# A fused attention and gated convolution kernel: q and k of group 5 loaded ahead of w_out, groups 3 to 5 run through the prologue, pair loop begun at group 6

## The chip, the cores and the metric

The kernel runs on one core of one Trainium2 chip. The metric is the device time of one execution in microseconds (us), where less is better. A run that lies more than 1.5% above the fastest of the same kernel is called slow here, and the other runs fast. Where the text says "span", it is the length of the profiled execution, about 1.8 us shorter than its device time (222.6 us for 224.45 in the profiled run of the kernel before).

## The reference, cut to what matters

```python
batch, n_heads, seq, head_dim = 8, 12, 448, 64         # d_model = 768
scores = q @ k.T / 8                                    # per batch and head, causal mask
attn   = softmax(scores) @ v                            # (8, 12, 448, 64)
x      = attn with heads joined                         # (8, 448, 768)
gate   = sigmoid(causal_depthwise_conv(x, conv_w))      # 5 taps
out    = (gate * (x @ w_val)) @ w_out                   # (8, 448, 768), float32
```

## The kernel before

The work is cut into 24 groups of four heads; three groups make one batch. For each group the kernel computes scores and exps in two stages, multiplies by v ("attention"), normalises, and runs the convolution that gives the gate. For each batch and each third of the columns there is a "value product" (`val`: x times w_val, times the gate), and for each pair of batches 14 "output tiles" (`project`: times w_out). Value products and output tiles have no fixed place: they fill the gaps in which TensorE would wait for ScalarE's exps. `plan` and `vals_in` say how many go into which gap. Names that end in `_ps` are the banks that TensorE writes its results to: `sc_ps` for scores and convolutions, `av_ps` and `den_ps` for attention and its denominators, `z_ps` and `den_ps` for products and output tiles.

Loads of q, k, w_val and w_out are issued by GpSimd, which also masks the exps with selects and casts v. Its timeline shows them in the order of the program, so a load behind a select waits for that select's exps: in the kernel before, a select starts at 38.63 us after 3.17 us of waiting for exps, and q of group 6, which the program has behind it, is issued at 43.35 us.

```python
    def next_outs(count, banks, tiles=1):     # output tiles; tiles=4 cuts each of the six matmuls into four narrow ones
        ...
    def first_half(n):
        if n < N:
            exps(n, 0)                        # scores on TensorE, exps on ScalarE, two selects on GpSimd
            transposes(n + 1)                 # q, k of the next group, on VectorE
            cast_v(n)                         # on GpSimd
            load_v(n + 3)
            for m in {4: (6, 7), 5: (8,), 6: (9,), 7: (10, 11)}.get(n, (n + 4,)):
                load_qk(m)                    # issued by GpSimd
    ...
    exps(2, 1, 2)
    load_qk(4)
    for c in range(NE):
        load_wo(c)                            # the six pieces of w_out
    load_qk(5)
    cast_v(1, nc.vector)
    load_v(4)
    values(1)                                 # attention and normalisation
    cast_v(2, nc.vector)
    load_v(5)
    conv((0, 1), sc_banks)
    values(2)
    transposes(3)
    next_val((z_ps, den_ps))
    exps(3, 0)
    next_val((z_ps, den_ps))
    conv((2,), [av_ps])
    exps(3, 1)
    ...
    plan = {2: (2, 0, 1, 0, 1), 3: (2, 0, 0, 0, 0), 4: (0, 1, 2, 1, 2), 5: (2, 0, 0, 0, 0)}
    vals_in = {2: (), 3: (2, 4), 4: (0,), 5: (2, 4)}
    for p in range(2, N // 2 + 1):            # one pair of groups per turn
        n = 2 * p
        ...
        first_half(n)
        gap(0, (den_ps, z_ps))
        second_half(n)
        values(n - 1)
        gap(1, (z_ps,), 4)                    # output tiles in gaps 1 and 3 are cut in four
        if p == 2:
            swap_wv()                         # an exchange of rows of w_val inside SBUF, four DMAs
        first_half(n + 1)
        gap(2, (den_ps, z_ps))
        second_half(n + 1)
        if n < N:
            values(n)
        gap(3, (z_ps,), 4)
        conv((n - 2, n - 1) if p > 2 else (n - 1,), sc_banks)
        gap(4, (den_ps, z_ps, av_ps[0]))
```

The softmax here doesn't subtract the row's maximum and nothing guards it: scores larger than these inputs give would overflow.

## Time and profile before

The time was 225.32 us, the median of three runs (224.0 to 225.81). The points below are the starts of a group's scores on TensorE and the end of the span, from the trace.

| point | us | stretch | us |
|---|---|---|---|
| scores of group 3 | 31.6 | start to group 3 | 31.6 |
| scores of group 6 | 52.3 | group 3 to 6 | 20.7 |
| scores of group 12 | 97.0 | group 6 to 12 | 44.7 |
| end of the span | 222.6 | group 12 to the end | 125.6 |

TensorE is busy 94% of the span, so the time is moved only by what makes TensorE stand, by its clock, or by more work. The list of TensorE's waits of this kernel gives, for each kind, the total in us, how many there were, and the longest. Two lines of it matter later.

```profile
PE sc_ps L181 <- ACT pt L190: 1.6, 5, 0.6
...
PE sc_ps L241 <- issue: 0.5, 1, 0.5
```

The first says that all waits of scores for ScalarE's exps together cost 1.6 us: the gaps are well filled. The second is one wait inside a convolution for which the profile names no other engine and no transfer ("issue").

### The profile page before, as it was taken

The numbers are of one execution on the slowest core, as the hardware profiler recorded it, in microseconds if no ns is written. First come the engines' busy times: TensorE is split into PE (matmuls) and PEld (weight loads), VectorE is DVE, ScalarE is ACT, GpSimd is POOL, SyncE is SP. The second block draws the span as 40 slices with busy tenths as digits, with TensorE's granted clock in tenths as the row PEclk, the third lists the DMA queues.
The fourth block names the chain that finished last, engine by engine and source line by source line (L and its number), as shares of the span: only waits on it lengthen the run. The fifth ranks groups of instructions, "written<-read, shape, count | busy, mean of one in ns | idle before, by whom it ended". The sixth has DMA issues, their size and how long they took to land.

```text
span 222.6 us, 8748 instructions
## 1 busy us (share of the span) xinstructions
PE 208.4 (94%) x3821; PEld 114.1 (51%) x3822; DVE 139.4 (63%) x251; ACT 139.7 (63%) x178; POOL 111.4 (50%) x192
## 2 busy tenths in 40 slices
PE   7997889987999999999999999999999999989992
PEld 3344434544455545545655655555555556546551
DVE  6747686558878754978828828749568476260400
ACT  2496316877666868667677777777677776406041
POOL 7299953893884736817717636557255155000000
PEclk9999699999999999999999999999999999999999
DMA  5999999899999885984885977758934210302333
GB/s 92 176 196 223 220 215 203 169 171 268 223 271 203 172 180 209 239 157 90 161 235 109 229 212 134 154 192 165 193 141 135 88 59 3 144 0 89 128 137 149
DMA packets 57696, 36.37 MB, mean 163 GB/s; under 512 B 46133, under 2 KB 54069, under 8 KB 57658
## 3 DMA queue, kind: packets, MB, share of 16 engines
q1 hardware_dynamic: 48922, 22.44, 37.6%
q0 software_dynamic: 8736, 13.37, 34.6%
q8 instruction: 30, 0.49, 0.9%
q14 instruction: 8, 0.07, 0.1%
HBM read 37.76 MB, written 11.01 MB: 219 GB/s over the span
## 4 chain that ended last, share of the span: by engine, by line
PE 77%; ACT 8%; DVE 7%; DMA 3%; issue 2%; POOL 1%; DVEq 0%; ACTq 0%; POOLq 0%
PE den_ps L263 12%; PE z_ps L263 11%; PE sc_ps L181 11%; PE z_ps L285 11%; ACT pt L190 7%; PE sc_ps L241 7%; PE den_ps L285 6%; PE av_ps L215 5%; PE den_ps L215 4%; PE av_ps L285 3%; PE z_ps L134 3%; DMA kb<-in_k_dram 3%; PE sc_ps L285 2%; DVE x L228 2%; DVE dt L222 1%
## 5 line engine op out<-in xcount | busy, mean ns | idle before, releaser
L190 ACT ACTIVATE pt<-sc_ps 128x1024 bf16<-128x1024 f32 x96 | 92.9, 1022 | 34.1 <-PE sc_ps L181 32.6
L194 POOL TENSOR_SCALAR_AFFINE_SELECT pt<-pt 128x512 bf16<-128x512 bf16 x24 | 16.0, 668 | 66.5 <-ACT pt L190 66.5
L285 PEld LDWEIGHTS <-gv 128*32 128x32 bf16 (+1 forms) x624 | 31.6, 97 | 22.3 <-issue 4.6
L263 PEld LDWEIGHTS <-wv 128*128 128x128 bf16 x288 | 26.4, 98 | 26.0 <-issue 3.2
L181 PE MATMUL sc_ps<-qt,kt 32*128 32x64 bf16 (+3 forms) x768 | 35.0, 277 | 2.1 <-ACT pt L190 1.6
L285 PE MATMUL z_ps<-wo,gv 128*32 128x384 bf16 (+1 forms) x462 | 33.2, 326 | 0.8 <-DVE gv L266 0.8
L200 POOL TENSOR_SCALAR_AFFINE_SELECT pt<-pt 128x512 bf16<-128x512 bf16 x48 | 30.2, 660 | 7.0 <-ACT pt L190 7.0
L181 PEld LDWEIGHTS <-kt 32*128 32x128 bf16 x768 | 18.4, 93 | 27.4 <-issue 17.2
L263 PE MATMUL z_ps<-x,wv 128*128 128x448 bf16 x138 | 30.2, 353 | 0.7 <-DVE x L228 0.7
L263 PE MATMUL den_ps<-x,wv 128*128 128x448 bf16 x138 | 30.3, 354 | 0.2
L266 DVE SCALAR_TENSOR_TENSOR gv<-gate,den_ps 128x448 bf16<-128x448 f32 x23 | 14.1, 612 | 24.6 <-PE den_ps L263 24.6
L228 DVE TENSOR_TENSOR x<-av_ps,rb 128x448 bf16<-128x448 f32 x48 | 27.7, 619 | 2.6
L248 ACT ACTIVATE gate<-sc_ps 128x896 f32<-128x896 f32 x23 | 19.9, 915 | 14.9 <-PE sc_ps L241 14.9
L222 DVE STREAM_TRANSPOSE dt<-den_ps 128x448 f32<-128x448 f32 x24 | 15.5, 644 | 18.4 <-PE den_ps L215 18.4
L215 PE MATMUL av_ps<-pt,vb 128*32 128x448 bf16 (+3 forms) x768 | 25.3, 274 | 0.7 <-DVE vb L86 0.7
L165 DVE STREAM_TRANSPOSE qt<-qb 128x448 uint32<-128x448 uint32 x24 | 22.8, 950 | 4.7 <-DMA qb<-in_q_dram 4.5
L290 ACT ACTIVATE ob<-z_ps 128x384 f32<-128x384 f32 x29 | 14.3, 493 | 15.8 <-PE z_ps L285 15.8
L165 DVE STREAM_TRANSPOSE kt<-kb 128x448 uint32<-128x448 uint32 x24 | 22.3, 930 | 1.8 <-DMA kb<-in_k_dram 1.8
L86 POOL CAST vb<-vf 128x1024 bf16<-128x1024 f32 x21 | 21.8, 1036 | 0.0
L215 PEld LDWEIGHTS <-vb 128*32 128x32 bf16 x768 | 16.3, 98 | 6.4 <-DVE vb L86 0.9
L241 PE MATMUL sc_ps<-x,cwd 32*32 32x448 bf16 x920 | 17.7, 369 | 1.8 <-DVE x L228 0.9
L266 DVE SCALAR_TENSOR_TENSOR gv<-gate,z_ps 128x448 bf16<-128x448 f32 x23 | 14.1, 614 | 7.9 <-PE z_ps L263 7.9
(46 smaller groups left out, 174.9 us busy)
## 6 DMA issues: line engine op xcount, KB each, us to landing
out_dram<-ob SPq DMA_DIRECT2D x27, 384.0 KB, 4.1
vf<-in_v_dram SPq DMA_DIRECT2D x72, 128.0 KB, 5.6
qb<-in_q_dram POOLq DMA_DIRECT2D x24, 224.0 KB, 4.8
kb<-in_k_dram POOLq DMA_DIRECT2D x24, 224.0 KB, 6.0
vf<-in_v_dram SPq DMA_DIRECT2D x24, 64.0 KB, 5.3
wv<-in_moe_w_val_dram POOLq DMA_DIRECT2D x12, 96.0 KB, 6.0
wo<-in_moe_w_out_dram POOLq DMA_DIRECT2D x6, 192.0 KB, 8.8
wv<-wv SPq DMA_DIRECT2D x4, 96.0 KB, 7.6
```

The lines of the kernel that those rows point to most:

```text
L86: engine.tensor_copy(out=t, in_=vfs.pop(n))
L165: nc.vector.transpose(out=t.bitcast(U32).rearrange("p (b s) -> p s b", s=T), in_=qks.pop((name, n)).rearrange("p s d -> p (s d)").bitcast( ...
L181: nc.tensor.matmul(out=sc_ps[h // 2][:, h % 2, c0:c0 + nq], lhsT=kt[r, e, k0:k0 + 128], rhs=qt[r, e, q0:S], start=e == 0, stop=e == 1, ski ...
L190: nc.scalar.activation(out=pt[:, 2 * hp:2 * hp + 2, 512 * stage:512 * (stage + 1)], in_=sc_ps[hp], func=AF.Exp, scale=D ** -0.5)
L200: nc.gpsimd.affine_select(out=pt[:, :, c:c + 128], in_=pt[:, :, c:c + 128], compare_op=ALU.is_ge, fill=0.0, base=0, pattern=[[0, G], [1, 1 ...
L215: nc.tensor.matmul(out=o, lhsT=w, rhs=pt[:, h, col:col + nq], start=i == 0, stop=i == 3, skip_group_check=True, tile_position=(0, 32 * i_out))
L228: nc.vector.tensor_tensor(out=x[:, dh, 4:S + 4], in0=av_ps[dh][:, 0:S], in1=r, op=ALU.mult)
L241: nc.tensor.matmul(out=banks[u][i // 2][32 * j:32 * (j + 1), 0:S], lhsT=cwd[r, 2 * version(n) + dh, t], rhs=xs[n % 8][r, dh, t:t + S], sta ...
L248: nc.scalar.activation(out=gates[n], in_=sc_ps[u][:, :, 0:S], func=AF.Tanh, scale=0.5)
L263: nc.tensor.matmul(out=o[e][:, 0:S], lhsT=wv_sb[version(NG * b + cg)][:, ce, f:f + 128], rhs=xs[(NG * b + cg) % 8][:, ce, 4:S + 4], start= ...
L266: nc.vector.scalar_tensor_tensor(out=gv[g][:, e, S * (b % 2):S * (b % 2 + 1)], in0=gates[NG * b + g][:, e], scalar=1.0, in1=o[e][:, 0:S], ...
L285: nc.tensor.matmul(out=o[w * j:w * (j + 1), 0:384], lhsT=gvs[p][g][:, dh, 128 * m + w * j:128 * m + w * (j + 1)], rhs=wo_sb[c][:, f], star ...
```

## The change

Its intent, as the code shows it: let q and k of group 5 arrive before w_out, run groups 3 to 5 straight through to their attention in the prologue, and let the regular loop begin at group 6. It also moves two v casts to other places and computes the last two of the six contraction steps of the first value product late.

```diff
-            for m in {4: (6, 7), 5: (8,), 6: (9,), 7: (10, 11)}.get(n, (n + 4,)):
+            for m in {6: (8, 9), 7: (10,), 8: (11, 12)}.get(n, (n + 4,)):
 ...
     load_v(3)
+    cast_v(1, nc.vector)
     exps(1, 1, 2)
     keep_clock(3)
+    exps(2, 0, 2)
     load_wvs(4)
-    load_qk(3)
-    exps(2, 0, 2)
     values(0)
     exps(2, 1, 2)
+    cast_v(2, nc.scalar)
+    load_qk(3)
     load_qk(4)
+    values(1)
+    conv((0, 1), sc_banks)
+    values(2)
+    transposes(3, v_f[1])
+    ...
+    next_val((z_ps, den_ps), 2)
+    conv((2,), [av_ps])
+    exps(3, 0)
+    transposes(4)
+    cast_v(3)
+    load_v(6)
+    load_qk(5)
+    next_val((z_ps, den_ps))
+    exps(3, 1)
     for c in range(NE):
         load_wo(c)
-    load_qk(5)
 ... (the old order of groups 1 to 3 removed)
     next_val((z_ps, den_ps))
+    exps(4, 0)
+    ...
+    values(3)
+    transposes(5)
+    exps(4, 1)
+    next_outs(1, (z_ps,))
+    exps(5, 0)
+    ...
+    load_qk(7)
+    values(4)
+    next_outs(1, (z_ps,), 4)
+    exps(5, 1)
+    transposes(6)
+    next_outs(2, (z_ps, den_ps))
+    values(5)
+    conv((3, 4), sc_banks)
+    swap_wv()
+    next_outs(1, (z_ps,))

-    plan = {2: (2, 0, 1, 0, 1), 3: (2, 0, 0, 0, 0), 4: (0, 1, 2, 1, 2), 5: (2, 0, 0, 0, 0)}
-    vals_in = {2: (), 3: (2, 4), 4: (0,), 5: (2, 4)}
-    for p in range(2, N // 2 + 1):
+    plan = {3: (0, 1, 0, 1, 2), 4: (1, 2, 0, 1, 1), 5: (0, 1, 0, 0, 0)}
+    vals_in = {3: (0, 2, 4), 4: (), 5: (0, 2)}
+    for p in range(3, N // 2 + 1):
```

## The prediction

> **What bounds the kernel now.** I read the page's head first: busy shares, then the forty slices of 5.6 us.
>
> ```profile
> PE 208.4 (94%) x3821; PEld 114.1 (51%) x3822; DVE 139.4 (63%) x251; ACT 139.7 (63%) x178; POOL 111.4 (50%) x192
> ...
> PE   7997889987999999999999999999999999989992
> ...
> PEclk9999699999999999999999999999999999999999
> DMA  5999999899999885984885977758934210302333
> ```
>
> TensorE is the bound at 94%. What it lacks lies in the first eleven slices and in the tail. Its clock fell once, in the fifth slice, and the DMA engines are full for the first 60 us. Next the order of instructions of both kernels: the first 17 us match on TensorE, and from the scores of group 12 (97.0 us of the span now) both have the same order to the end, with 8 value products and 14 output tiles done by then. So the remaining 125.5 us are the same work, and the change can only move the moment at which group 12 begins.
>
> Then the timeline of TensorE from 17 to 55 us, where the idle time before a piece is in brackets.
>
> ```profile
> 21.21 1.06 PE L215 MATMUL av_ps<-pt,vb 128*32 128x448 bf16 x32 [0.71 <-DVE vb L86]
> ...
> 23.45 2.59 PE L241 MATMUL sc_ps<-x,cwd 32*32 32x448 bf16 x79 [0.89 <-DVE x L228]
> ...
> 31.62 0.63 PE L181 MATMUL sc_ps<-qt,kt 32*128 32x448 bf16 x16
> ...
> 39.42 1.17 PE L285 MATMUL den_ps<-wo,gv 128*128 128x384 bf16 x6 [0.18 <-DVE gv L266]
> ...
> 51.21 1.14 PE L285 MATMUL den_ps<-wo,gv 128*128 128x384 bf16 x6 [1.20 <-DVE dt L222]
> 52.28 0.64 PE L181 MATMUL sc_ps<-qt,kt 32*128 32x448 bf16 x16
> ```
>
> The gaps that the change aims at: 0.71 us for the cast of v, 0.89 us for x of group 1, and 1.20 us at 51.2, whose releaser stood behind the k transpose of group 6. The lines at 31.62 (group 3 starts), 39.42 (first output tile) and 52.28 (group 6 starts) are my reference points. The windows of 3.4 us around the clock's fall:
>
> ```profile
> 20.40:23.80 3.40, 1.80 (x49) 0.87 (x42) 3.23 (x7) 0.56 (x1) 3.40 (x7) 1.00 1.19 230
> 23.80:27.20 3.40, 3.25 (x103) 1.77 (x98) 1.33 (x3) 1.10 (x2) 3.40 (x7) 0.50 1.19 214
> ```
>
> After a window with TensorE 53% busy (1.80 of 3.40) comes one at clock 0.50, and then 1.00 again: 1.7 us of work lost. Last, the DMA issues. These two are the sixth w_out piece (issued 30.57) and k of group 5 (issued 33.65), from narrow windows:
>
> ```profile
> wo<-in_moe_w_out_dram POOLq DMA_DIRECT2D x1, 192.0 KB, 9.7
> ```
> ```profile
> kb<-in_k_dram POOLq DMA_DIRECT2D x1, 224.0 KB, 9.1
> ```
>
> So w_out is complete at 30.57 + 9.7 = 40.3 us, just when the first output tile, at 39.42, comes to its sixth matmul. w_out is not early in the old kernel; it is just in time. k of group 5 stands behind it and lands at 33.65 + 9.1 = 42.8; its transpose holds TensorE for 0.30 us at 43.8. That is what the reordering of the loads can win directly.
>
> [...] the DMA share is 1.16 to 1.22 in every 5 us stretch from 20 to 40. [...]
>
> **The change, part by part.**
>
> *Early waits.* The second v cast moves ahead of the first normalisation on VectorE (its data are there: 0.9 MB had moved on the v queue by 15 us) and the third goes to ScalarE, where a 128x1024 pass takes 1.02 us and which is free after 20.9. That removes the 0.71 us wait and brings x of group 1 forward by about 0.6. x of group 2 then comes near 27.7 instead of 29.9, and computing the last two of six contraction steps late hides what remains. But group 3 cannot start before its k is here. On GpSimd, q and k of group 3 now stand behind two more selects (0.63 + 0.41 and 1.2 us) and a later w_val: sel(2) from 20.1, four w_val issues of 0.55 to 23.3, sel(2) to 24.5, then q at 24.5, k at 25.05. k needs at least 4.0 us (what k of group 0 took on empty queues), more likely 5, plus 0.95 for its transpose: group 3 starts at 30.2 to 31.3, I take 30.9 against 31.62. The convolution of group 2 (1.1 us) is done before it instead of after. Gain here: 0.7 + 1.1 = 1.8 us.
>
> *q, k ahead of w_out.* This is the step that decides. GpSimd is in order. Group 3's scores at 30.9, exps on ScalarE done at 30.9 + 2.7 = 33.6, two selects to 34.65, cast (1.04) to 35.65, and only then q and k of group 5 (now 32.3 and 33.65). Second scores at 30.9 + 0.6 + 2.4 (a value product is 1.24 + 1.14) = 33.9, exps to 36.6, selects to 37.9, then six w_out issues of 0.54: 37.9 to 41.2, against 27.1 to 31.1 now. Meanwhile the software queue has nothing between k of group 4 (about 32) and 37. k of group 5, issued at 36.2 with 4.3 to 5.8 us to land (its range on lightly loaded queues in this trace), is here near 41; w_out follows at the pace of now, where k of group 4 landed at 26.57 + 6.6 = 33.2 and w_out was complete 7.1 us later. So w_out is complete near 48.1, between 46 and 50.
>
> TensorE reaches the first output tile after scores, value product, scores, value product, scores (30.9 to 37.5), attention of group 3 (1.5, with a short wait for its selects) and the second scores of group 4, held by the exps to 40.2. It stands from 40.2 to about 48.3, less the matmuls whose weights have come: 7 us idle. The clock goes to half, and comes back one busy window later: 1.5 us more.
>
> *From the first output tile to group 6.* Scores 0.6, attention 1.42, output 1.03, scores 0.6, two outputs 2.1, attention 1.42 after 0.8 of waiting for the denominator bank (its copy stands behind two exps on ScalarE), convolution 1.24, output 1.03: 10.2 us. Group 6 starts at 48.3 + 10.2 + 1.5 = 60.0, against 52.28. By then one attention (1.42) and one output tile (1.03) more are done, 2.5 us.
>
> *Group 6 to group 12.* Now 44.8 us with about 1.4 us of short waits. Afterwards 2.5 us less work, but the places between two users of the score banks are filled less: scores of group 9 follow each other with nothing between (two exps of 1.02 less 0.3: 1.7 us), the convolution of groups 8 and 9 is followed at once by scores (two gates, 1.73 us), and four further places have one output tile of 1.03 where 1.7 to 2 are to be covered (0.6 to 0.9 each, 3 in all). That is 6.4 us of waits for 1.4. So 44.8 - 2.5 + 5 = 47.3, and group 12 starts at 107.3 instead of 97.0.
>
> Sum by terms: early gain -1.8, stall +7 (arrival at the tile is already 0.8 later because 2 us of work and some waits now stand before it), clock +1.5, thinner filling +5, removal of the old waits between 42 and 52 (0.3 + 0.6 + 1.2) -2.1: +9.6 us by terms, +10.3 by the walk. Every wait in it is taken at its full length, and hand walks add up waits that in fact overlap (a later TensorE finds ScalarE done), so I take three quarters: +7.5, that is 232.8 us.
>
> **The rivals.**
>
> *The early gain stands and w_out is in time.* Speaking for it: somebody placed the output tiles and chose the new plan with care, and the loads of v for groups 4 and 5 are held back on purpose by a dependence on the q transpose of group 3, which frees DMA time. Against it: all issues on GpSimd stand behind selects that wait for exps of group 3. Even with every step at its shortest (k landing in 4.0 us, w_out at 1 us a piece) w_out is complete at 45.3 and the tile is reached at 39.1. If I am wrong nonetheless, 1.8 + 2.1 us are won: 221 to 222 us.
>
> *The stall comes but is given back.* TensorE stands, the DMA queues run ahead, later waits go. Against: from 97 us on TensorE is at 20.00 of 20.00 in four stretches of 20 us, so there is no slack to give back; only the 1.4 us between groups 6 and 12 could be. Time about 227 to 229.
>
> *ScalarE becomes the bound between groups 6 and 12*, because scores, gates and output copies meet with no other TensorE work between. It is 63% busy; it holds TensorE only at the six places counted. With the full sum: 235.
>
> **Range and chances.** The shortest variant of each step gives a stall of 5 us and half of the thinner filling: +2 to +4, 228. The longest gives w_out at 50 and two cold windows: +13, 238. Range 226.5 to 238. The threshold for slower is 229.8. I give slower 0.73, same 0.17, faster 0.10; the last two are for the case that my order of GpSimd's work or the pace of its queue is wrong, and for the care that the author evidently took.
>
> **What would show it.** The chain of waits should hold a DMA of w_out at 40 to 48 us; the timeline of TensorE a wait of several us inside the first output tile's six matmuls, with a clock of 0.5 after it; w_out's first issue at 37 to 38.5; group 6's scores starting near 58 to 60 and group 12's at 102 to 107; waits of about 1.5 us on exps and gates at group 9's second and group 12's first scores; from group 12 to the end 125.5 us as before. It would be wrong if w_out is complete by 42, or if group 12 starts before 98.

## The result, and the profile after

The changed kernel took 247.85 us (median of four runs, 244.75 to 250.73) against 224.84 us (224.0 to 225.81) of the kernel before: a ratio of 1.093, with a 95% interval of 1.0814 to 1.1046. It is slower, by about 21 to 23 us. A ratio is the mean time of one kernel's fast runs over that of the other's fast runs in the same rounds, so it is not quite the ratio of the medians quoted beside it. The first profile of the changed kernel fell on a slow run, so I ran the same kernel again (run `after_again`, 246.38 us, ratio 1.0924), and all lines of the changed kernel below are from that profile of a fast run.

The head of the page of the changed kernel:

```profile
PE 216.0 (88%) x3893; PEld 116.1 (47%) x3894; DVE 138.9 (57%) x251; ACT 141.8 (58%) x180; POOL 111.0 (45%) x192
...
PE   7896986388996977995999988999999999998993
...
PEclk9999999759997999999799999999999999999998
DMA  5999998967559539979179398487792430111324
```

TensorE has 72 more matmuls than before (3893 for 3821) and 72 more weight loads, and is busy 88% instead of 94%. A slice is now 6.1 us. The row PE shows a 3 in the eighth slice (43 to 49 us), and PEclk a 7, 5 there and after it, and further 7s in the 13th and the 20th slice. DMA is nearly full through the eighth slice and then falls to 3 and 1 in places.

GpSimd's timeline of the changed kernel (start, length, and in brackets the idle time before with what ended it):

```profile
34.78 0.63 POOL L197 TENSOR_SCALAR_AFFINE_SELECT pt<-pt 128x512 bf16<-128x512 bf16 x1 [7.01 <-ACT pt L193]
...
37.26 0.54 POOL L67 DMA_DIRECT2D kb<-in_k_dram  x1
...
38.97 3.20 POOL L105 DMA_DIRECT2D wo<-in_moe_w_out_dram  x6
```

GpSimd stood idle for 7 us, waiting for the exps of group 3, and the loads behind that select waited with it. The six w_out issues begin at 38.97 us; before, the first five began at 27.09. TensorE's timeline of the changed kernel has the price:

```profile
31.95 0.63 PE L184 MATMUL sc_ps<-qt,kt 32*128 32x448 bf16 x16 [0.74 <-DVE kt L168]
...
44.78 0.32 PE L290 MATMUL z_ps<-wo,gv 128*128 128x384 bf16 x1 [3.57 <-DMA wo<-in_moe_w_out_dram]
...
49.88 0.48 PE L290 MATMUL z_ps<-wo,gv 128*128 128x384 bf16 x1 [0.70 <-DMA wo<-in_moe_w_out_dram]
...
63.26 0.37 PE L184 MATMUL sc_ps<-qt,kt 32*128 32x448 bf16 x2
...
115.25 0.37 PE L184 MATMUL sc_ps<-qt,kt 32*128 32x448 bf16 x2 [1.01 <-ACT gate L251]
```

In the kernel before, group 12 started so:

```profile
97.01 0.64 PE L181 MATMUL sc_ps<-qt,kt 32*128 32x448 bf16 x16
```

These lines answer the reference points of the prediction. Group 3 starts at 31.95 us (31.62 before). TensorE reaches the first output tile at 41.2 (44.78 less the 3.57 of waiting), and its sixth matmul begins only at 49.88. Group 6 starts at 63.26 (52.28 before), group 12 at 115.25 (97.01 before). About a microsecond of such a difference can be chance: the idle matmuls ahead of group 1's scores, where all programs of this document are still equal, continue at 10.88 us in the profile of the kernel before, at 11.96 in this one, and between 10.8 and 12.3 in all 18 profiles. The DMA issue view of a narrow window around the last two w_out pieces of the changed kernel gives, at the end of the line, the us to landing:

```profile
wo<-in_moe_w_out_dram POOLq DMA_DIRECT2D x2, 192.0 KB, 7.9
```

and that around k of group 5:

```profile
kb<-in_k_dram POOLq DMA_DIRECT2D x1, 224.0 KB, 5.9
```

So k of group 5 is here at 37.26 + 5.9 = 43.2 us, about when it came before (42.8). The 7.9 is a median of two; the last piece, issued at 41.6, took 8.2 us, so w_out is complete at 49.8 instead of 40.3. The reordering won nothing for k and delayed w_out by more than nine microseconds.

The clock, in windows of the changed kernel (start and end, length, busy time of TensorE, weight loads, VectorE, ScalarE and GpSimd with instruction counts, granted TensorE clock, DMA share, GB/s):

```profile
44.20:47.60 3.40, 1.28 (x3) 0.30 (x3) 0.00 (x0) 0.00 (x0) 2.22 (x4) 0.73 1.15 206
47.60:51.00 3.40, 2.08 (x11) 0.50 (x14) 0.00 (x0) 0.49 (x1) 0.00 (x0) 0.50 1.15 204
51.00:54.40 3.40, 3.40 (x68) 2.02 (x64) 1.87 (x4) 1.94 (x2) 0.89 (x2) 0.50 0.55 118
...
117.30:120.70 3.40, 3.40 (x14) 1.15 (x15) 0.76 (x2) 1.43 (x2) 1.84 (x3) 0.52 0.00 0
```

The clock is at half behind the stall (0.50 from 47.6 to 54.4 us), as in the old kernel behind the window that ends at 23.8 us (0.50). But a second stretch at half clock comes at 117 us (0.52), where both kernels run the same order. The list of TensorE's waits of the changed kernel shows what is behind it:

```profile
PE z_ps L290 <- DMA wo<-in_moe_w_out_dram: 6.4, 6, 3.6
PE sc_ps L244 <- issue: 3.0, 3, 1.3
PE sc_ps L184 <- ACT pt L193: 2.7, 4, 1.2
PE den_ps L218 <- DVE gv L271: 2.3, 2, 2.1
PE sc_ps L184 <- ACT gate L251: 2.3, 4, 1.0
```

The w_out stall is 6.4 us. The waits for exps and gates (2.7 and 2.3; before, 1.6 and none) are the thinner filling. The second and fourth lines the prediction has no step for.

*The second line.* Three convolutions stop in their middle, with nothing in the trace that they wait for:

```profile
113.87 0.36 PE L244 MATMUL sc_ps<-x,cwd 32*32 32x448 bf16 x3 [1.07 <-issue]
...
147.99 0.37 PE L244 MATMUL sc_ps<-x,cwd 32*32 32x448 bf16 x5 [1.29 <-issue]
...
179.83 0.56 PE L244 MATMUL sc_ps<-x,cwd 32*32 32x448 bf16 x19 [0.61 <-issue]
```

Counting pairs of a weight load and a matmul in the trace, these are the 1627th, 2267th and 2907th pair (the expectations below count 11 more for the same places). They lie 640 pairs apart, which is five times 128. In the kernel before, the one such wait stands at the 1243rd pair, three times 128 pairs ahead of the 1627th. An instruction queue has nearly the same period: it moves 30 packets of 16,384 bytes in both executions (30 packets, 0.49 MB on the page), and from the first packet to the last TensorE passes 126.9 pairs for each in the kernel before, and 127.0 in the first profile of the changed kernel. So I estimate that one packet holds 128 pairs, and I call the end of such a stretch a border; it is what the expectations below call 16 KB of program. The packets take 0.9 to 1.3 us each here, and one starts at 111.4, one at 145.7 and one at 177.6 us, that is 1.0 to 1.6 us before one of these three waits begins and 2.2 to 2.4 us before it ends. That TensorE waits there for the instructions of the packet is my inference from these times.

All the traces together make this firmer. In the 16 whose matmul records are complete, I matched the packets with every 128th pair, 464 borders in all. At 30 of them TensorE waits for "issue", up to 1.5 us, and each of these waits ends 2.2 to 2.6 us after the border's packet starts. At the other 434 the packet had started at least 2.3 us earlier. So in these traces a border shows where its packet starts late, and this is mostly where TensorE runs through a block quickly: 27 of the 30 waits follow 128 pairs that took 3.1 to 3.6 us, convolutions among them. What sets the start of a packet, the traces do not say.

*The fourth line.* VectorE's timeline of the changed kernel at group 7:

```profile
73.41 0.97 DVE L168 STREAM_TRANSPOSE qt<-qb 128x448 uint32<-128x448 uint32 x1 [4.55 <-DMA qb<-in_q_dram]
74.96 0.95 DVE L168 STREAM_TRANSPOSE kt<-kb 128x448 uint32<-128x448 uint32 x1 [0.59 <-DMA kb<-in_k_dram]
75.76 0.60 DVE L271 SCALAR_TENSOR_TENSOR gv<-gate,den_ps 128x448 bf16<-128x448 f32 x1
```

The new table asks for q and k of group 8 only in the first half of group 6, and GpSimd issued them at 68.78 and 69.33 us; they landed at 73.3 and 74.9. VectorE reached their transposes long before they came, and the product that empties the denominator bank stands behind the transposes. TensorE waited 2.13 us for that bank until 76.41, and its clock was at 0.50 in the window behind it (76.5 to 79.9 us).

### The profile page after: what moved, and what is told of

Its sections match the earlier page's. It is cut to its first block, busy times and chain, and to the rows that moved or that the text cites. A ratio compares the mean times of both kernels' runs of the same rounds, so it can differ in the third digit from the quotient of the medians.

```text
span 247.1 us, 8892 instructions
## 1 busy us (share of the span) xinstructions
PE 216.8 (88%) x3893; PEld 116.2 (47%) x3894; DVE 139.0 (56%) x251; ACT 141.5 (57%) x180; POOL 111.5 (45%) x192
## 4 chain that ended last, share of the span: by engine, by line
PE 69%; DMA 8%; ACT 7%; POOL 5%; issue 5%; DVE 4%; SPq 0%; POOLq 0%; DVEq 0%; ACTq 0%
PE z_ps L290 11%; PE den_ps L267 9%; PE sc_ps L184 9%; PE z_ps L267 9%; PE av_ps L218 7%; PE sc_ps L244 6%; PE den_ps L218 5%; ACT pt L193 4%; PE den_ps L290 4%; DMA wo<-in_moe_w_out_dram 4%; PE av_ps L290 3%; DMA kb<-in_k_dram 2%; PE sc_ps L290 2%; POOL wv L97 2%; ACT gate L251 2%
## 5 line engine op out<-in xcount | busy, mean ns | idle before, releaser
L290 PE MATMUL z_ps<-wo,gv 128*32 128x384 bf16 (+1 forms) x552 | 39.4, 336 | 9.2 <-DMA wo<-in_moe_w_out_dram 7.6
L184 PE MATMUL sc_ps<-qt,kt 32*128 32x64 bf16 (+3 forms) x768 | 36.1, 279 | 5.7 <-ACT pt L193 3.2
L295 ACT ACTIVATE ob<-z_ps 128x384 f32<-128x384 f32 x32 | 15.7, 491 | 29.4 <-PE z_ps L290 29.4
L267 PE MATMUL den_ps<-x,wv 128*128 128x448 bf16 x138 | 31.5, 362 | 0.2
L267 PE MATMUL z_ps<-x,wv 128*128 128x448 bf16 x138 | 31.3, 362 | 0.3 <-DVE x L231 0.2
L251 ACT ACTIVATE gate<-sc_ps 128x896 f32<-128x896 f32 x22 | 19.0, 914 | 18.1 <-PE sc_ps L244 18.1
L218 PE MATMUL av_ps<-pt,vb 128*32 128x448 bf16 (+3 forms) x768 | 26.9, 285 | 0.0
L244 PE MATMUL sc_ps<-x,cwd 32*32 32x448 bf16 x880 | 16.9, 371 | 5.2 <-issue 3.6
L218 PE MATMUL den_ps<-pt,ones 128*32 128x448 bf16 (+3 forms) x384 | 16.6, 289 | 4.0 <-DVE gv L271 2.3
L218 PEld LDWEIGHTS <-vb 128*32 128x32 bf16 x768 | 17.1, 101 | 6.1 <-issue 0.9
## 6 DMA issues: line engine op xcount, KB each, us to landing
qb<-in_q_dram POOLq DMA_DIRECT2D x24, 224.0 KB, 4.5
kb<-in_k_dram POOLq DMA_DIRECT2D x24, 224.0 KB, 5.7
```

What stands on the lines that cost most here:

```text
L184: nc.tensor.matmul(out=sc_ps[h // 2][:, h % 2, c0:c0 + nq], lhsT=kt[r, e, k0:k0 + 128], rhs=qt[r, e, q0:S], start=e == 0, stop=e == 1, ski ...
L218: nc.tensor.matmul(out=o, lhsT=w, rhs=pt[:, h, col:col + nq], start=i == 0, stop=i == 3, skip_group_check=True, tile_position=(0, 32 * i_out))
L244: nc.tensor.matmul(out=banks[u][i // 2][32 * j:32 * (j + 1), 0:S], lhsT=cwd[r, 2 * version(n) + dh, t], rhs=xs[n % 8][r, dh, t:t + S], sta ...
L251: nc.scalar.activation(out=gates[n], in_=sc_ps[u][:, :, 0:S], func=AF.Tanh, scale=0.5)
L267: nc.tensor.matmul(out=o[e][:, 0:S], lhsT=wv_sb[version(NG * b + cg)][:, ce, f:f + 128], rhs=xs[(NG * b + cg) % 8][:, ce, 4:S + 4], start= ...
L290: nc.tensor.matmul(out=o[w * j:w * (j + 1), 0:384], lhsT=gvs[p][g][:, dh, 128 * m + w * j:128 * m + w * (j + 1)], rhs=wo_sb[c][:, f], star ...
```

## The experiments

The table is read from the traces: the start of the first exp of a group on ScalarE, and the span, in us.

| run | group 3 | group 6 | group 12 | group 18 | end |
|---|---|---|---|---|---|
| kernel before | 32.4 | 53.0 | 97.8 | 145.1 | 222.6 |
| changed kernel (after_again) | 32.7 | 64.8 | 116.8 | 167.1 | 245.6 |
| w_out_early | 32.5 | 59.8 | 111.5 | 160.4 | 238.5 |
| plain_tiles | 32.8 | 63.8 | 114.2 | 161.8 | 239.3 |
| plan_refilled | 32.2 | 64.3 | 108.8 | 156.4 | 233.9 |
| w_out_and_plan | 34.1 | 59.7 | 103.4 | 150.8 | 228.3 |
| before_narrow | 34.1 | 54.7 | 100.0 | 148.8 | 227.1 |

One per cent of the kernel before is 2.25 us, and I call it a point below. The kernels ran in four batches, each with its own runs of the kernel before, whose medians were 224.6 to 225.7 us. The theory after the result was that four things add up: late w_out, thinner filling, the half clock after the stall, and late q and k of group 8. The rival was that one cause, the stall, sets off the others. All kernels gave the right result.

### First batch: one part undone at a time

**w_out_early.** The changed kernel with w_out asked for where it was before, ahead of q and k of group 5.

```diff
     load_qk(4)
+    for c in range(NE):
+        load_wo(c)
     values(1)
 ...
     exps(3, 1)
-    for c in range(NE):
-        load_wo(c)
```

> The changed kernel with the six loads of w_out put back to directly behind q and k of group 4; nothing else. If the late w_out is the main cause: w_out is complete near 40.5 us, the first output tile waits under 1 us instead of about 8, q and k of group 5 then hold group 5's scores to about 44.7, group 6 starts near 55.5 instead of 64.0, and the time falls by about 8.5, to 237 to 240 us. If instead the stall were only hiding a wait for something else (k of group 5, or a loop that is short of work anyway), the time falls by under 4 us.

It took 240.46 us, ratio 1.0634 [1.0551, 1.0716]. Against the changed kernel's 1.0924 that is 2.9 points, 6.5 us, where 8.5 had been expected. TensorE's timeline of this run shows that another load took part of the place of w_out:

```profile
45.35 1.04 PE L184 MATMUL sc_ps<-qt,kt 32*128 32x448 bf16 x16 [3.31 <-DVE kt L168]
```

These are the scores of group 5. They wait 3.31 us for k of group 5, which is issued at 37.08 us behind a select and a cast and lands 7.2 us later.

**qk_ahead.** The changed kernel with q and k of group 8 asked for in the prologue.

```diff
-            for m in {6: (8, 9), 7: (10,), 8: (11, 12)}.get(n, (n + 4,)):
+            for m in {6: (9, 10)}.get(n, (n + 4,)):
 ...
     load_qk(7)
+    load_qk(8)
     values(4)
```

> The changed kernel with q and k of group 8 asked for in the prologue directly behind group 7, and groups 9, 10, 11 then one group earlier each. If the short lookahead of the new load table is what stopped TensorE at 75 to 77 us: the wait of 2.1 us before group 6's attention and the half-clock stretch that follows it (1.7 us lost) are gone, 3 to 4 us less, 243 to 244. If that wait was only an echo of the stall at 40 to 51 us, which this leaves in: under 1 us less.

It took 250.8 us, ratio 1.1099 [1.102, 1.1177]: slower than the changed kernel, against my theory. TensorE's timeline of this run says most of why:

```profile
73.61 0.55 PE L267 MATMUL den_ps<-x,wv 128*128 128x448 bf16 x2 [4.22 <-DMA wv<-wv]
```

The exchange of w_val's rows inside SBUF now runs next to the new loads. Its median landing time is 8.9 us instead of 4.6 (first profile of the changed kernel), and the value product waits 4.22 us for it. The wait on k of group 8 was removed and a longer one put in its place. Not all of this profile's delay is due to it: group 3 already starts 2.4 us later than in the changed kernel, where the programs are equal, because VectorE waited 4.36 us for v of group 1.

**plan_refilled.** The changed kernel with the output tiles put elsewhere: none in gaps where they are cut in four, two where TensorE otherwise waits for exps.

```diff
-    plan = {3: (0, 1, 0, 1, 2), 4: (1, 2, 0, 1, 1), 5: (0, 1, 0, 0, 0)}
-    vals_in = {3: (0, 2, 4), 4: (), 5: (0, 2)}
+    plan = {3: (0, 1, 0, 0, 0), 4: (2, 0, 2, 0, 2), 5: (2, 0, 0, 0, 0)}
+    vals_in = {3: (0, 2, 4), 4: (), 5: (2, 4)}
```

> The changed kernel with the output tiles and value products of groups 6 to 11 spread as the kernel before has them for its loop (two tiles or a product between two users of the score banks; same counts at group 12). If the thinner filling costs what the prediction said (about 5 us) the waits on exps and gates between 87 and 117 us (1.2, 0.6, 0.6, 1.0, 0.4 us) go and the time falls by 4 to 5 us, to 242 to 243. If the waits overlap with other limits: 1 to 2 us.

It took 235.78 us, ratio 1.0465 [1.0408, 1.0523]: 4.6 points or 10.3 us better than the changed kernel, twice the 5 us that I had set for thinner filling. From group 6 to 12 it takes 44.5 us instead of 52.0, but it also wins after group 12, 125.1 us instead of 128.8, where its order is that of the changed kernel. It has 3821 matmuls, as many as the kernel before, because fewer output tiles are cut in four. That observation started the second theory: that the number of instructions ahead of a place matters.

**warm_fillers.** The changed kernel with 44 idle matmuls ahead of the first output tile, to keep the clock up through the stall.

```diff
     exps(4, 1)
+    keep_clock(44)
     next_outs(1, (z_ps,))
```

> The changed kernel with 44 matmuls on a zero tile ahead of the first output tile, about 9.5 us that TensorE would spend waiting for w_out anyway. w_out is as late as before. If the half clock after the stall is a cost of its own: clock 1.0 from 51 us on, group 6 starts 3 us earlier, time 3 to 5 us less, 242 to 245. If only the wait itself counts: no change, or up to 1 us slower if the fillers end after w_out has come.

It took 244.75 us, ratio 1.0753 [1.0659, 1.0846], and its profile fell on a slow run. The gain of 1.7 points can't be put down to the clock: the 44 extra pairs also move every later instruction against the borders; its trace has two such waits, of 1.02 and 2.99 us. This run is inconclusive, and warm_aligned below replaces it.

### Second batch: the number of instructions, and parts together

**plain_tiles.** The changed kernel, with the output tiles in the early gaps not cut in four. The work and its places are the same, and the 72 extra pairs of instructions are gone.

```diff
-        gap(1, (z_ps,), 4)
+        gap(1, (z_ps,), 4 if p > 4 else 1)
 ...
-        gap(3, (z_ps,), 4)
+        gap(3, (z_ps,), 4 if p > 4 else 1)
```

> The changed kernel with four of its output tiles (in the two trips of the loop for groups 6 to 9) computed with six matmuls instead of 24 narrow ones; same work, same order, 72 matmuls and weight loads fewer, so that TensorE's program has as many instructions as before. Theory A: the waits named issue inside the convolutions, which stand in three runs at the same instructions (1638, 2278, 2918 of TensorE's pairs, all the same modulo 128, that is 16 KB of program), are waits for the next 16 KB of instructions, and the longer program put these borders inside the convolutions. Then those waits (3.6 us in the changed kernel) and the half clock after the first of them (1.7 us) go: 240 to 242 us. Theory B: they come from something else in these convolutions: they stay, and the time stays at 245 to 248.

It took 241.4 us (241.02 to 241.70), ratio 1.0721 [1.0659, 1.0782]. That is 2.0 points (4.6 us) better than the changed kernel. A tile takes 1.15 us in either form (24 or 6 matmuls), so it is not the tile itself. The page of this run has the counts of the kernel before:

```profile
PE 212.8 (89%) x3821; PEld 114.7 (48%) x3822; DVE 138.6 (58%) x251; ACT 141.5 (59%) x180; POOL 111.1 (46%) x192
```

The three waits inside convolutions are gone, and so is the stretch at half clock at 117 us, where the two halves of the value product took 1.67 and 2.45 us in the changed kernel and take 1.31 and 1.30 here:

```profile
114.04 1.31 PE L267 MATMUL den_ps<-x,wv 128*128 128x448 bf16 x6
115.19 1.30 PE L267 MATMUL z_ps<-x,wv 128*128 128x448 bf16 x6
```

From group 12 to the end it needs 125.0 us by the exps of the table, as the kernel before does within 0.3. One wait of 0.45 us without a cause remains, inside an output tile at 104 us.

**w_out_and_plan.** Both edits of the first batch that helped, together (the diffs of w_out_early and plan_refilled).

> w_out asked for early and the loop filled as before, both in one. If the two costs are separate they add: 246 less 6 to 8 less 10 is 228 to 230 us, and the wait for q and k of group 8 (2 us before group 6's attention) is what is left, with one half-clock stretch. If they overlap (the fill gave its gain because the stall had been there): 232 to 234.

It took 229.64 us, ratio 1.018 [1.0104, 1.0256]. From plan_refilled that is 2.85 points for w_out, the same as from the changed kernel: the two terms add. What is left is 1.8 points; the record classes it as "unclear" for its threshold of 2%, but the interval lies above 1. The wait behind k of group 8 has shrunk in this trace, from 2.13 to 0.55 us, though its loads were not moved.

**four_undone.** As that, and q and k of group 8 ahead, and the exchange issued early.

```diff
     load_v(7)
+    swap_wv()
     load_qk(6)
 ...
     conv((3, 4), sc_banks)
-    swap_wv()
```

> As the last, with q and k of group 8 asked for one step earlier as well and the exchange of the w_val halves issued before it, so that it doesn't stand in the DMA queues behind them. If the short lookahead is the third cost, the 2 us wait before group 6's attention is gone: 2 to 4 us less than the run with two, 225 to 227 us. If the wait only moves to the exchanged w_val (as it did with the lookahead alone): as the run with two, or slower.

It took 228.74 us, ratio 1.016 [1.0097, 1.0222], the same as w_out_and_plan within the intervals, and not the 225 to 227 hoped for: only 0.55 us of the wait behind group 8 had been left to win. The wait for k of group 5 is still there (2.99 us).

**early_part_alone.** The kernel before with the early part of the change alone: both casts moved, the first value product's last two steps late.

```diff
     load_v(3)
+    cast_v(1, nc.vector)
     exps(1, 1, 2)
 ...
     exps(2, 1, 2)
+    cast_v(2, nc.scalar)
     load_qk(4)
 ...
-    cast_v(1, nc.vector)
     load_v(4)
     values(1)
-    cast_v(2, nc.vector)
     load_v(5)
 ...
-    next_val((z_ps, den_ps))
+    next_val((z_ps, den_ps), 2)
```

> The kernel before with only the early part of the change: second cast of v ahead of the first normalisation, third on ScalarE, the last two contraction steps of the first value product late. Prediction's early gain: the 0.71 us wait for the cast goes, x of group 2 comes 0.6 us or more earlier, 0.7 to 1.8 us faster than before, 223 to 224.5. If group 3's k is what sets the start of group 3 in either case: no change within 0.5 us.

It took 225.58 us, ratio 1.0026 [0.9956, 1.0095]: no gain. TensorE's timeline of this run shows what group 3 waits for once the earlier waits are gone:

```profile
31.30 0.63 PE L184 MATMUL sc_ps<-qt,kt 32*128 32x448 bf16 x16 [0.89 <-DVE kt L168]
```

The scores of group 3 start at 31.30 us instead of 31.62, after 0.89 us of waiting for the transpose of k. In this run the transpose of k sets that point, and not the waits that are gone.

### Third batch: the opposite direction

**before_narrow.** If the number of instructions matters, adding the same 72 pairs to the kernel before must cost. It cuts four of its output tiles in four and changes nothing else.

```diff
-        gap(0, (den_ps, z_ps))
+        gap(0, (den_ps, z_ps), 4 if p == 3 else 1)
 ...
-        gap(2, (den_ps, z_ps))
+        gap(2, (den_ps, z_ps), 4 if p == 4 else 1)
```

> The kernel before with four output tiles (two before group 6's second scores, two before group 9's) computed with 24 narrow matmuls instead of six: same work and order, 72 more matmuls and weight loads, so that from group 10 on TensorE's program is as far along as in the changed kernel. If the borders of 16 KB of program are what stops the convolutions: waits named issue of 0.5 to 1.5 us at TensorE's pairs 2278 and 2918 (about 150 and 180 us before the shift of the span), which the kernel before doesn't have, and 1.5 to 3 us slower, 226.5 to 228. If they belong to the changed kernel's late loads or its stall: no such waits, 225 within 0.5.

It took 227.7 us, ratio 1.0126 [1.0084, 1.0169], 2.8 us slower. TensorE's timeline of this run has waits that the kernel before does not have:

```profile
129.62 0.37 PE L241 MATMUL sc_ps<-x,cwd 32*32 32x448 bf16 x5 [1.31 <-issue]
...
161.39 0.55 PE L241 MATMUL sc_ps<-x,cwd 32*32 32x448 bf16 x19 [0.54 <-issue]
```

They stand at the 2267th and 2907th pair, exactly where the changed kernel has its second and third, though 18 us earlier; a third, of 1.21 us, stands at the 987th, in a value product. So the place in the program, not the time, decides. Waits of this kind add up to 3.1 us here and 3.0 in the changed kernel. Of the 4.5 us by which this profile is longer, 1.7 lie before group 3, ahead of the edit; from there to the end it takes 2.8 us more, as the ratio says.

**warm_aligned.** Idle matmuls ahead of the first output tile again, with output tiles left uncut so that the later instructions keep their places.

```diff
     exps(4, 1)
+    keep_clock(36)
     next_outs(1, (z_ps,))
 ... (the four tiles of plain_tiles uncut, and two more)
```

> The kernel with plain tiles (241.4 us) plus 36 matmuls on a zero tile, 7.8 us, ahead of the first output tile, and two more plain tiles, so that the program stays as long as before. w_out is as late. If the half clock is a cost of its own: clock 1.0 after the stall, 2.5 to 3.5 us less, 238 to 239. If the half clock runs where TensorE waits anyway: within 1 us of 241.4.

It took 240.56 us, ratio 1.0708 [1.0655, 1.0761]. Its comparison is plain_tiles (1.0721), and the intervals overlap: the two differ by 0.3 us, give or take about 1.8. So the half clock after the stall is not told apart from zero, nor from the predicted 1.5 us. TensorE's timeline of this run shows that the stall was filled nearly to its end:

```profile
42.99 7.72 PE L137 MATMUL z_ps<-idle 128*128 128x512 bf16 x35 [0.16 <-issue]
...
52.51 0.32 PE L290 MATMUL z_ps<-wo,gv 128*128 128x384 bf16 x1 [0.78 <-DMA wo<-in_moe_w_out_dram]
```

The clock was full afterwards: the next 16 matmuls of scores took 0.63 us, where those after the stall of the changed kernel took 1.04. From the scores of group 5 to those of group 6 it took 10.5 us instead of the 11.8 of plain_tiles, 1.3 us less. In the span this does not show, because group 3 starts 1.7 us later in this profile, ahead of the edit.

**qk6_early.** The kernel before with q and k of group 6 asked for directly behind those of group 5, aimed at its own 1.20 us wait at 51 us.

```diff
-            for m in {4: (6, 7), 5: (8,), 6: (9,), 7: (10, 11)}.get(n, (n + 4,)):
+            for m in {4: (7,), 5: (8, 9), 6: (10,)}.get(n, (n + 4,)):
 ...
     load_qk(5)
+    load_qk(6)
```

> The kernel before with q and k of group 6 asked for in the prologue, directly behind group 5 (and groups 8 to 10 not moved or one step earlier), which keeps w_out where it is. The wait of 1.2 us at 51.2 us, which stands behind group 6's k transpose, should go: 0.8 to 1.3 us faster, 223.7 to 224.2. If another wait takes its place: no change within 0.5 us.

Its runs fall in two levels, three at 223.79 to 224.69 us and three at 228.0 to 228.6; the ratio of the fast ones is 0.9987 [0.9943, 1.0031]. No gain, and more spread. I did not find out what decides between the levels.

**best_try.** qk6_early with the early part, and q and k of group 3 asked for ahead of four pieces of w_val.

```diff
-    load_wvs(4)
     load_qk(3)
+    load_wvs(4)
 ... (and the edits of qk6_early and early_part_alone)
```

> As the last, with the early part of the change, and with q and k of group 3 asked for ahead of the last four pieces of w_val, because with the early part alone group 3's start waited 0.9 us for its k. Group 3 then starts near 29.5 to 30 instead of 31.6 and the 1.2 us wait is gone: 2 to 3 us faster than before, 222 to 223. If the w_val pieces come too late for the first value product: no gain over the last run.

It took 227.5 us, ratio 1.0077 [1.0022, 1.0132]. Its profile, of a slow run, has a wait of 2.56 us for the exchange of w_val's rows.

### Fourth batch: what was still open

Three questions were open: how far the result repeats (after_again, told above: 1.0924 [1.0853, 1.0995]), whether both orders of w_out and k of group 5 can be had at once, and whether the exchange stands in the way of earlier loads.

The expectation of after_again was:

> The changed kernel as it is, for runs of both states and a profile to set beside the others: 244 to 251 us again. If the borders of program in the convolutions make it uneven, its fast runs spread over more than 3 us, where the same work with plain tiles spread over 0.7.

Its fast runs spread over 3.3 us (244.03 to 247.35), as expected. But those of the kernel before, in the same batch, spread over 3.2 us (223.72 to 226.93), with one border wait of 0.5 us. So the spread is no evidence for the borders.

**both_early.** The changed kernel with q, k of group 5 and then w_out all directly behind q, k of group 4, with the plan refilled and the exchange early.

```diff
     load_qk(4)
+    load_qk(5)
+    for c in range(NE):
+        load_wo(c)
     values(1)
 ... (both removed below, plan and exchange as in four_undone)
```

> What the change's intent needs, with nothing held back: q and k of group 5 directly behind group 4's, w_out directly behind them, all issued before group 3's selects; the loop filled as before, the exchange of w_val early. If only w_out's place behind the selects made it late: w_out is complete near 43, 2.7 us (two transfers) later than with w_out first, the first output tile waits 2 to 3 us, and k of group 5 no longer does: 227.5 to 229.5, as the run with four undone (228.7). If the DMA queue has room after all: 226 or less.

It took 232.91 us, ratio 1.0354 [1.0289, 1.0419]: slower than w_out_and_plan, and than either expectation. TensorE's timeline of this run:

```profile
42.72 0.32 PE L290 MATMUL z_ps<-wo,gv 128*128 128x384 bf16 x1 [0.70 <-DMA wo<-in_moe_w_out_dram]
...
46.39 0.99 PE L218 MATMUL den_ps<-pt,ones 128*32 128x320 bf16 x12 [2.13 <-POOL pt L203]
```

Now w_out costs 1.0 us in two waits, and a wait of 2.13 us for a select on GpSimd comes on top; the wait behind k of group 8 is 1.99 us again. In this profile, of the fastest of its runs, group 6 starts at 59.1 us, 0.6 earlier than in w_out_and_plan. The DMA share is 0.87 to 1.17 in every 5 us from 30 to 50, and GpSimd is busy for 4.87 of the last 5. I read it so: with both that full, the order of the loads decides what is waited for more than how long. No run tests this reading.

**qk_ahead_swap_early.** qk_ahead with the exchange issued early, as in four_undone.

> The changed kernel with the longer lookahead that cost 4 us instead of winning 3, now with the exchange of the w_val halves issued before that transfer. If the exchange landing late (8.9 us instead of 4.6) was what took the gain: its wait of 4.2 us goes and with it the time falls by 4 us or more against the lookahead alone (250.8), to 243 to 247. If the loss lay in the early stretch: stays at 249 to 252.

It took 243.66 us, ratio 1.0805 [1.0727, 1.0884]: 1.2 points better than the changed kernel and 2.9 better than qk_ahead. So the exchange was what had spoiled qk_ahead; from group 6 to 12 this profile takes 49.2 us, where qk_ahead's takes 54.4. It also means that the late q and k of group 8 are worth up to 1.2 points in the changed kernel, though the interval nearly reaches zero. In the company of early w_out and a refilled plan they were worth 0.2.

**best_exchange_early.** best_try with the exchange issued right behind the loads of v of group 6.

```diff
     load_v(6)
+    swap_wv()
 ...
-        if p == 2:
-            swap_wv()
```

> The kernel before with early part, q and k of groups 3 and 6 earlier, and the exchange of w_val early as well. The wait of 2.6 us for the exchange, which made the last try slower, should go; then 1 to 2 us faster than before, 223 to 224. If the DMA queues are simply full until 60 us, another wait replaces it: 225 to 226.

It took 224.78 us, ratio 0.9975 [0.9919, 1.0031], 1.0 point better than best_try and the same as the kernel before. No version that I ran beats the kernel before beyond its interval.

## Why the prediction was right or wrong

The direction and the first mechanism were right; the time was not. 232.8 us were predicted with a range to 238, and 246 to 248 were measured. The ratios divide the loss like this, in points of 2.25 us. They are differences of ratios from different batches, so each has an uncertainty of about one point.

| term | from | to | points |
|---|---|---|---|
| w_out late, with the half clock behind it | 1.0924 (changed) | 1.0634 (w_out_early) | 2.9 |
| thinner filling, groups 6 to 12 | 1.0721 (plain_tiles) | 1.0465 (plan_refilled) | 2.6 |
| 144 more TensorE instructions | 1.0924 (changed) | 1.0721 (plain_tiles) | 2.0 |
| the rest | 1.0180 (w_out_and_plan) | 1 | 1.8 |

That w_out adds to the plan is shown by the pair plan_refilled to w_out_and_plan, again 2.85 points. The sum is 9.3.

**Early gain (predicted -1.8 us).** Wrong in size, as far as the runs can tell. early_part_alone is 0.3% slower, with an interval that holds zero. "group 3 starts at 30.2 to 31.3, I take 30.9": it started at 31.95 in the profile of the changed kernel, after 0.74 us of waiting for its k. Chance is larger than this miss: in the eight profiles whose programs equal the changed kernel up to there, group 3 starts between 31.10 and 34.33 us, and in the three that equal the kernel before, between 31.62 and 33.30. One reading was wrong in each of the eight: for the second v cast, "its data are there". The 0.9 MB that the queue had moved did not hold all of v of group 1, and VectorE waited 1.0 to 4.4 us for it; in the changed kernel:

```profile
16.34 0.69 DVE L89 CAST vb<-vf 128x1024 bf16<-128x1024 f32 x1 [1.34 <-DMA vf<-in_v_dram]
```

With other waits ahead of group 3 removed, its scores waited for k instead: 0.74 us in the changed kernel, 0.89 in early_part_alone.

**The stall on w_out (predicted +7, w_out complete "near 48.1", tile reached at 40.2).** Right. TensorE reached the tile at 41.2, w_out was complete at 49.8, and the waits sum to 6.4 us. Undoing it wins 6.5 us. This win is net of the 3.31 us that k of group 5 costs when w_out goes first.

**The clock (predicted +1.5).** Right in kind: it fell to 0.5 after the stall. Its worth is not settled: the ratio of warm_aligned tells it apart neither from zero nor from 1.5 us, and its profile gives 1.3 us. The prediction counts on the fall from one window, 53% busy (1.80 of 3.40 us) with 0.50 behind it; other windows as busy had no fall behind them (see the last section).

**From the tile to group 6 (predicted 60.0).** It came at 63.26. Of the 3.3 us, 2.0 are the later end of the stall (50.3 for 48.3), and 1.3 lie in the stretch itself, 13.0 us for 11.7, which ran at less than full clock up to the window that ends at 57.8 (0.50 from 51.0 to 54.4, 0.77 after).

**Thinner filling (predicted +5 us, group 6 to 12 in 47.3).** The term itself was right: 2.6 points are 5.8 us. But the stretch took 52.0 us, because the prediction's walk had no wait for q and k of group 8 (2.13 us, with a window at half clock behind it) and none for a border in the program (1.07 us). It saw the new table of loads in the diff and did not ask when GpSimd would reach the loads.

**"From group 12 to the end 125.5 us as before."** This is the step that failed worst. It took 130.3 us by the scores, and 128.8 for 124.8 by the exps of the table. I argued from the order of instructions, "both have the same order to the end ... so the remaining 125.5 us are the same work". The order and the work are the same, but 144 more TensorE instructions ahead of it had shifted the borders. The shift put borders into convolutions, which then stood 1.07, 1.29 and 0.61 us, the first of them just ahead of group 12; and behind a short run of waits around it (1.07, 1.01 and 0.43 us between 113 and 116 us) the clock was at 0.52 for one window. Removing the 72 pairs (plain_tiles) brought the stretch back to 125.0 us by the exps, and adding 72 to the kernel before cost 1.26%. That the count of instructions matters is shown in both directions. That it acts through the instruction packets is inferred from the traces: the waits stand multiples of 128 pairs apart, and each ends 2.2 to 2.6 us after a packet of 16,384 bytes starts. No run changed the packets themselves.

**"I take three quarters."** Wrong. Summed by terms the prediction had +9.6 and by the walk +10.3, and took +7.5 on my estimate that the waits would overlap. The two largest terms did not overlap; they added, as the pair of w_out and plan shows. Even the walk in full would have been 12.8 us too low on the span. Held against the points of the trace, 1.0 of it had arisen by the start of group 3 (no more than chance, as said above), another 1.0 by the end of the stall, 1.3 by group 6, 4.7 by group 12 and 4.8 after it. So three quarters of the error lie after group 6. Two small slips decide nothing: the DMA shares from 20 to 40 us are 1.16 to 1.21, and group 6 to 12 took 44.7 us before.

**The rivals.** "w_out is in time" and "the stall is given back" both fell. For the third, ScalarE as the bound between groups 6 and 12, I had written 235; the waits for exps and gates sum to 5.0 us in the changed kernel, as that rival had them, but the sum of the rest was larger.

**What stays open.** In the trace of w_out_and_plan the wait for k of group 5 is 2.6 us long, which would be 1.2 of the last 1.8 points; that is an inference, because no kernel that ran took this wait away without setting another in its place. The rest of the 1.8 is not explained. The fast runs of the changed kernel spread over 3.3 us and those of plain_tiles over 0.7; since those of the kernel before spread over 3.2 us in one batch, the borders are not shown to be the reason. The half clock after the stall is counted with w_out in the table; alone it was not told apart from noise.

## What to carry to other kernels

Before moving a load, write down when the engine that issues it will reach that place in its own program: here GpSimd was waiting for exps, and a load that was "moved behind" two others came more than nine microseconds later. Equal order of instructions from some point on did not mean equal time here (128.8 us for 124.8 from group 12 on); count the instructions ahead of it too, and look for waits without a cause at regular distances (here multiples of 128 pairs). A new order of the loads changed what was waited for: asking for q and k of group 8 earlier removed a wait of 2.13 us and brought one of 4.22 us for the exchange. So test it together with every other transfer of that stretch.

## What was not expected of the hardware

- 144 more instructions on TensorE, 1.9% of its program, cost 2.0 points in one kernel and 1.3 in another, with no more time spent in the work itself.
- A wait of 1.07 us next to two others (1.01 and 0.43) lay ahead of a window at clock 0.52 at 117 us; the window before that one was 58% busy (1.96 of 3.40 us, 113.9 to 117.3). In the kernel before the clock fell after a window that was 53% busy (20.4 to 23.8 us); in plain_tiles it did not fall after one of 53% (87.8 to 91.2 us), nor in the first profile of the changed kernel after one of 58% (111.3 to 114.7 us). I looked at windows of 3.41 us, on the grid on which the clock changes in the traces, in all 18 of them, where the clock was full: after each of the 21 windows in which TensorE was busy for 46% or less it fell to 0.5, after none with 60% or more, and in between it fell after 11 and not after 18.
- At 30 of 464 borders TensorE waited, up to 1.5 us, and each of these waits ended 2.2 to 2.6 us after the start of the border's packet; at the other 434 the packet had started at least 2.3 us earlier. At three borders of the changed kernel the cost was 0.61 to 1.29 us.
- An exchange inside SBUF of four 96 KB pieces took 4.6 us to land in the first profile of the changed kernel, 5.8 in four_undone, 7.6 in the kernel before and 8.9 in qk_ahead (medians). Earlier loads of q and k alone gave a ratio of 1.1099 (qk_ahead), and 1.0805 with the exchange issued before them (qk_ahead_swap_early).
- A load of 224 KB took 4.0 us to land for k of group 0 in the kernel before, with only q of its group ahead of it. For k of group 5, among other transfers, it took 5.9 us in the changed kernel, 7.2 in w_out_early and 9.1 in the kernel before.
